# Linear attention with a gated output layer: a new order of TensorE work, loads parted from transposes, six output row buffers and a tail stored by two queues

## The chip, the cores and the metric

The kernel runs on one core of one Trainium2 chip. The metric is the device time of one execution in microseconds (us). The kernel before takes 238.62 us, the median of three timed runs (236.26 to 238.75). A single-core run is marked fast here when it lies within 1.5% of the fastest run of the same kernel in the same set, otherwise slow; a kernel run only once has no mark.

## The reference, cut to what matters

There are two parts. The first is linear attention, for 8 batches with 8 heads, 576 positions and head size 64. The second is a gated output layer of width 512 on its result.

```python
def phi(x):                                      # (b, h, 576, 64) -> (b, h, 576, 256)
    proj = np.einsum('bhsd,df->bhsf', x, w_phi)
    proj = proj - np.max(np.abs(proj), axis=-1, keepdims=True)
    return np.concatenate([np.exp(proj), np.exp(-proj)], axis=-1)
q_p, k_p = phi(q), phi(k)
kv  = np.einsum('bhsf,bhsd->bhfd', k_p, v);  z = np.sum(k_p, axis=2)
num = np.einsum('bhsf,bhfd->bhsd', q_p, kv)
den = np.einsum('bhsf,bhf->bhs', q_p, z)[..., None] + 1e-06
x   = (num / den).transpose(0, 2, 1, 3).reshape(8, 576, 512)
# gated layer: a causal convolution of 5 taps over positions gates x @ w_val
gate = sigmoid(sum over the taps of conv_w[k] * x shifted)
out  = (gate * (x @ w_val)) @ w_out
```

## The kernel before

The program is a list of some 1,040 tasks, one group of instructions each, written down in an order that was found beforehand (`ORDER`). Each engine carries out its own tasks strictly in that order. So a task that waits for a transfer holds up all later tasks of its engine.

For every batch from 2 on, GpSimd issues two loads, k and q (576 KB each). SyncE then issues a DMA transpose of each of them. The attention part projects k and q (`kp`, `qm`, `qp`), builds `kv` (`st`) and divides (`num`, `nrm`). Its result `XN` has to be transposed to `XT` for the gated part (`gate`, `val`, `out`). The batches in `XB` let a DMA do that, the others use TensorE and a copy by VectorE.

```python
XB = (3, 4, 5, 6, 7)                             # x is transposed by DMA in these batches
...
bufs = TT("KQN", 3, [P, NC, 2 * D])              # k and q as loaded: three buffers in turn
for b in range(1, B):
    for i, w in enumerate("kq"):
        self.N[w][b] = bufs[(2 * b + i) % 3]
...
def load(self, t, w, b):                         # GpSimd issues the loads of k and q
    o = self.N[w][b][:, :, :].rearrange("p y c -> p (y c)")
    ...
    self.nc.gpsimd.dma_start(o, self.rows(w, b))

def xpose(self, t, w, b):                        # SyncE issues their transposes
    self.nc.sync.dma_start_transpose(
        self.XT_[w][b % 2][:, :].rearrange("p (y c) -> p y c", c=P),
        self.N[w][b][:, :, :].rearrange("p y c -> p (y c)"))
...
def xtd(self, t, b, i):                          # x transposed by DMA
    self.nc.sync.dma_start_transpose(self.XT[b % 2][:, :, i, HALO:HALO + P], ...)

def xtp(self, t, b, i):                          # ... or by TensorE; i == 2 are the tail rows
    if i < 2:
        for h in range(H):
            nc.tensor.transpose(ps[:, h * P:(h + 1) * P], ..., self.ident[:, :])
    else:                                        # 16 transposes of 32x32
        for hh in range(4):
            for g in range(2):
                for par in range(2):
                    nc.tensor.transpose(ps[par * D:(par + 1) * D, hh * 32:(hh + 1) * 32], ...)
...
self.OUTS = TT("OUTS", 4, [P, DM], FP32)         # output rows: four buffers

def odma(self, t, b, c):                         # c == 4: the tail rows of two batches
    O = self.OUTS[out_seq(b, c) % 4]
    ...
        for i in range(2):
            for a in range(2):
                nc.sync.dma_start(d, O[p0:p0 + 32, :])
```

Of the kernel before, what the change touches and what calls it, by code (L numbers as in the profile page):

```python
# [26 lines left out]
XB = (3, 4, 5, 6, 7)  # L27
PIECES = 4
# [5 lines left out]
    "9:7:5 23:7:1 77:3:1 "  # L34
# [6 lines left out]
    "0 1 2 4 3 6 5 8 7 10 21 9 23 12 11 22 25 43 13 24 45 27 20 47 156 18 26 29 48 46 14 164 41 28 19 157 297 49 44 59 16 15 "  # L41
    "30 60 50 51 37 52 42 62 17 39 38 61 176 40 53 55 177 81 56 33 63 54 31 82 34 35 58 32 83 77 165 84 36 57 78 158 79 159 "
    "160 80 75 161 181 76 185 162 183 301 298 186 64 85 65 184 170 86 163 187 182 197 168 200 71 171 188 99 169 166 302 100 "
    "87 199 167 66 88 299 198 212 101 213 300 89 220 90 70 91 218 221 67 179 219 193 92 68 69 216 195 178 93 217 214 95 180 "
    "215 96 196 303 94 194 189 97 72 190 222 304 73 98 172 223 74 307 191 308 102 192 104 103 173 201 110 105 310 208 227 111 "
    "114 229 115 340 309 341 108 419 228 224 207 109 116 225 319 117 346 106 347 321 112 107 203 338 226 113 339 322 420 230 "
    "209 231 320 118 311 174 210 202 314 305 211 119 232 312 315 175 120 121 122 316 313 342 123 124 343 204 306 318 323 205 "
    "421 325 125 206 317 126 324 128 127 344 129 326 345 233 422 130 133 235 348 131 327 349 134 234 329 236 132 353 238 135 "
    "354 137 237 136 423 355 328 429 138 251 424 432 350 252 148 351 430 140 545 352 149 334 330 141 431 433 331 546 434 241 "
    "332 245 139 242 425 435 239 549 246 441 436 333 426 240 247 444 437 248 243 439 144 244 443 438 249 550 356 145 442 547 "  # L50
    "440 152 357 250 253 335 254 153 255 445 358 336 548 446 427 259 337 447 150 460 260 461 256 448 261 257 464 258 362 465 "
    "270 364 363 466 271 359 268 428 467 360 551 262 361 269 462 263 463 555 264 365 557 142 265 366 146 151 266 558 468 154 "
    "272 469 552 267 556 377 449 470 274 451 471 378 478 273 371 480 275 143 367 667 372 147 277 479 671 368 155 588 475 450 "
    "278 668 589 369 477 279 373 285 476 374 455 280 379 286 567 380 586 370 569 472 375 587 474 289 276 376 381 672 473 281 "
    "290 456 293 570 282 291 669 559 294 568 385 292 562 388 386 382 387 560 389 383 670 452 390 553 384 590 295 453 591 561 "
    "481 563 482 454 457 564 394 283 554 483 287 458 395 565 594 459 398 566 595 484 399 571 396 485 673 296 572 486 592 397 "
    "284 573 391 575 593 487 288 574 581 392 493 674 393 488 677 489 494 679 400 793 490 680 681 401 495 491 684 794 678 596 "
    "402 411 683 577 492 597 685 496 407 412 688 682 497 598 499 576 600 408 415 498 500 409 599 403 686 413 416 501 578 404 "
    "502 503 687 712 601 713 410 797 579 603 582 414 708 580 507 795 602 798 709 504 508 505 510 796 509 716 506 511 717 714 "
    "512 689 675 715 513 692 405 610 514 417 611 690 516 515 612 710 517 691 607 711 693 695 522 608 676 694 520 523 696 609 "  # L60
    "604 521 583 799 697 803 606 518 804 406 605 584 519 418 806 703 585 807 537 800 808 805 619 525 620 810 704 621 538 526 "
    "615 809 622 527 815 616 817 718 915 613 528 719 625 524 614 818 720 919 916 626 811 617 722 533 698 816 813 541 623 618 "
    "534 721 726 812 699 529 728 542 627 814 628 530 840 624 727 629 732 841 705 733 838 920 706 839 734 729 917 707 836 731 "
    "700 837 842 701 918 730 843 723 702 801 834 725 639 835 640 633 724 630 641 844 631 845 634 819 632 743 820 635 741 802 "
    "744 821 846 742 822 735 848 747 736 745 737 847 748 849 738 642 746 851 739 636 643 850 749 637 750 925 740 638 921 929 "
    "751 926 646 823 932 829 644 922 647 927 648 645 531 928 930 933 825 539 936 752 535 649 532 923 753 931 934 755 540 824 "
    "754 958 756 536 959 935 764 924 757 858 765 956 830 859 758 957 761 860 759 762 960 760 826 961 763 852 941 827 853 942 "
    "766 828 943 854 770 767 944 855 771 962 857 831 963 937 832 856 938 768 833 964 655 769 939 965 869 945 940 651 946 870 "
    "656 966 861 652 657 863 967 862 653 873 772 977 543 864 658 951 968 978 874 663 654 952 979 867 865 947 659 970 544 777 "
    "660 868 866 969 773 661 650 971 664 774 662 948 972 778 665 974 871 949 973 666 953 950 975 775 875 872 980 876 954 981 "  # L70
    "877 789 976 955 776 781 982 985 782 989 790 783 991 990 791 785 784 986 983 786 992 881 887 984 993 995 792 882 996 888 "
    "884 883 987 994 878 889 885 879 997 880 894 779 998 988 886 999 787 890 895 780 896 891 788 892 1006 893 1003 897 1000 "
    "1007 898 1009 1008 1001 1010 1004 911 1005 1002 899 1011 912 1016 900 913 1018 1017 901 914 1012 902 1014 1013 1019 907 "
    "1015 903 908 1020 909 1021 904 905 1033 1022 910 1023 1025 1034 906 1035 1029 1024 1037 1030 1036 1026 1031 1027 1038 "
    "1032 1039 1028 1040 "
)
FLEX = (
    "ADAADDAADDPPDPPDDADDAADDDDPPDPPDADADAPPAPPDADAAPPDPPDADDDDPPDPPDDAAAPPDPPADDAADPPDPPAAAAAPPDPDDAADAA"
)
BANKS = (  # L80
    "015441025023012345670167010123676742367672367672302301130167016723230167233424745010167230145452345010123234544567016745"
    "456752323550167452323452301232310245234567014567230167452350101230145010106723176745012323016701675674670101670101232367"
    "016767667454545236723452376723674501674501234005145676745452323236723014562345674545672323011230145012323014545540101450"
    "123674501010167670102367452367670101673452345452323012367047660167674523674501674523016456745010167232323067452301674545"
    "232316702367016723234567670123010676701452301230145467456701234501452377660"
# [69 lines left out]
def build(plan, em=None):  # L155
# [11 lines left out]
    def G(*k):  # L167
        return h.get(k)
# [4 lines left out]
    for b in range(B):  # L173
# [18 lines left out]
        for w in "kq":  # L192
            if b == 0:
                continue
            ld = A("l" + w, b, 0, "POOL", 0.75, fn("load", w, b), (seq[-3] if len(seq) >= 3 else []) + [hold[b] if b < 2 else None],
                   rank=-500 + (w == "q") if b == 1 else -980 if b == 0 else None, lat=0.6)
            h["ld" + w] = ld
            xf = A("l" + w, b, 0, "DMA", 3.8 if w == "k" else 3.5, None, [ld])
            dp = [xf]
            if w == "k":  # L200
                dp += [G("kp", b - 2, u) for u in range(NU)]
            else:
                dp += [G("qp", b - 2, u) for u in range(NU)] + [G("qm", b - 2, u) for u in range(NU)]
            if 0 < b <= PEB:
                tps = []
                for i, (c0, n) in enumerate(((0, 8), (8, 8), (16, 2))):
                    g = plan.group("tp", 1)
                    tp = h["sx" + w, b] = A("x" + w, b, i, "PE", 0.06 * n, fn("tp16", w, b, c0, n), dp, g, 0)
                    tps.append(tp)
                    x = A("x" + w, b, i, ("DVE", "ACT"), (dve(n * P), act(n * P)), fn("tc16", w, b, c0, n), [tp], g)  # L210
                    for u, (d0, m) in enumerate(UNITS):
                        if c0 <= d0 < c0 + n:
                            h["x" + w, b, u] = x
                seq.append(tps)
                continue
            x = h["sx" + w, b] = A("x" + w, b, 0, "SP", 2.7, fn("xpose", w, b), dp, rank=-700 if b == 0 else None, lat=-1.5)
            x = A("x" + w, b, 0, "DMA", 3.2, None, [x])
            seq.append([x])
            for u in range(NU):
                h["x" + w, b, u] = x  # L220
        if b == 1:
            cl = A("lk", 0, 0, "POOL", 1.7, fn("c_ld"), [hold[1]], rank=-450, lat=0.6)
            cx = A("lk", 0, 0, "DMA", 6.8, None, [cl], rank=-450)
            cd = A("lk", 0, 0, "SP", 0.8, fn("c_dup"), [cx], rank=-440)
            cx = A("lk", 0, 0, "DMA", 1.7, None, [cd], rank=-440)
# [595 lines left out]
```

## Time and profile before

| | before |
|---|---|
| timed runs, median | 238.62 us |
| the profiled run (marked slow) | 250.01 us, span 248.2 us |
| TensorE idle in its span | 248.2 - 206.3 = 41.9 us |
| mean granted TensorE clock | 0.928 |

The lines that the prediction rests on stand in it, with their reading. Two more views belong to the argument. The first is the list of DMA issues of the kernel before; the last number of a line is the median time in us from issue to landing:

```profile
KQN<-in_q_dram POOLq DMA_DIRECT2D x7, 576.0 KB, 11.3
...
XT<-XN SPq DMA_TRANSPOSE x10, 4.8
...
kT<-KQN SPq DMA_TRANSPOSE x6, 11.4
```

The second is the timeline of GpSimd and of SyncE's queue in the middle of the kernel before (start, duration, then what was issued):

```profile
70.50 0.60 POOL L497 DMA_DIRECT2D KQN<-in_q_dram  x1
...
69.23 5.13 SPq L512 DMA_TRANSPOSE qT<-KQN  x1
74.45 8.49 SPq L512 DMA_TRANSPOSE kT<-KQN  x1
```

The q load (70.50 us) is in flight while a q and a k transpose are carried out (69.23 to 82.94). The issue of one k transpose alone occupies SyncE's queue for 8.49 us.

### The profile page before, as it was taken

How to read it: one execution, taken by the hardware profiler on the slowest of the kernel's cores; microseconds unless marked ns; L12 is line 12 of the kernel's file. 1: busy time of each engine (PE TensorE's matmuls, PEld its weight loads, DVE VectorE, ACT ScalarE, POOL GpSimd, SP SyncE). 2: the span in 40 equal slices, each digit the busy share in tenths (PEclk: the TensorE clock that was granted, in tenths of full speed). 3: DMA queues.
4: the chain of work that ended last, by engine and by line, in shares of the span. 5: the costliest groups of instructions: out<-in, count | busy, mean ns of one | idle time of the engine just before them, and what ended most of it. 6: DMA issues, size and time to landing. Idle time of an engine off the chain costs nothing.

```text
span 248.2 us, 9200 instructions
## 1 busy us (share of the span) xinstructions
PE 206.3 (83%) x4033; PEld 144.7 (58%) x4047; DVE 173.8 (70%) x266; ACT 178.6 (72%) x258; POOL 102.2 (41%) x153
## 2 busy tenths in 40 slices
PE   6768877869979799997999898608999999799990
PEld 3545556646665577576665664504767876467640
DVE  2897799964786699968998789602898995264220
ACT  3888898977977586897899889801888969341440
POOL 5303999910980008902671079000087096001010
PEclk9995799997997999999999999955999999799998
DMA  6998978996599996999999999999498039284245
GB/s 211 322 223 128 191 224 132 203 263 103 87 138 154 206 241 156 208 209 278 163 187 99 313 168 136 76 54 296 45 212 260 3 115 168 66 136 123 85 145 151
DMA packets 55617, 41.43 MB, mean 167 GB/s; under 512 B 40026, under 2 KB 44890, under 8 KB 55514
## 3 DMA queue, kind: packets, MB, share of 16 engines
q1 hardware_dynamic: 49568, 31.46, 59.0%
q0 software_dynamic: 5760, 9.31, 26.0%
q8 instruction: 31, 0.51, 0.9%
q10 hardware_dynamic: 250, 0.09, 0.1%
q14 instruction: 8, 0.07, 0.1%
HBM read 30.49 MB, written 9.44 MB: 161 GB/s over the span
## 4 chain that ended last, share of the span: by engine, by line
PE 52%; DMA 13%; ACT 13%; DVE 12%; issue 7%; SPq 0%; ACTq 0%; DVEq 0%
PE PS L722 11%; PE PS L746 8%; DMA XT<-XN 7%; PE PS L703 7%; ACT QTIL L626 6%; PE PS L567 5%; PE PS L524 5%; ACT KTIL L541 5%; DMA out_dram<-OUTS 4%; PE PS L639 4%; DVE XN L660 3%; DVE MK L531 3%; PE PS L611 3%; PE PS L710 3%; PE PS L618 2%
## 5 line engine op out<-in xcount | busy, mean ns | idle before, releaser
L557 POOL TENSOR_TENSOR VT<-VN,EK 128x1152 bf16<-128x1152 f32 x31 | 65.8, 2123 | 55.5 <-ACT EK L550 42.6
L541 ACT ACTIVATE KTIL<-PS 128x1024 bf16<-128x1024 f32 (+1 forms) x80 | 73.5, 954 | 8.4 <-PE PS L524 5.4
L626 ACT ACTIVATE QTIL<-PS 128x1024 bf16<-128x1024 f32 x64 | 63.3, 1034 | 9.0 <-PE PS L618 6.8
L531 DVE TENSOR_REDUCE MQP<-PS 128x8 f32<-128x1024 f32 (+1 forms) x40 | 44.2, 1114 | 17.4 <-PE PS L524 14.6
L531 DVE TENSOR_REDUCE MK<-PS 128x8 f32<-128x1024 f32 (+1 forms) x40 | 44.1, 1111 | 5.2 <-PE PS L524 2.7
L714 ACT ACTIVATE TH<-PS 128x576 bf16<-128x576 f32 x32 | 19.9, 650 | 26.7 <-PE PS L710 25.9
L722 PE MATMUL PS<-XT,WV 64*128 64x288 bf16 x512 | 35.7, 283 | 0.2 <-DVE GV L728 0.2
L746 PE MATMUL PS<-WOUT,GV 128*128 128x512 bf16 x116 | 31.3, 395 | 1.0 <-issue 0.5
L728 DVE SCALAR_TENSOR_TENSOR GV<-TH,PS 128x576 bf16<-128x576 bf16 x32 | 23.7, 751 | 10.8 <-PE PS L722 10.1
L567 PE MATMUL PS<-VT,KTIL 64*128 64x65 bf16 x1152 | 25.5, 193 | 6.3 <-issue 5.9
L722 PEld LDWEIGHTS <-WV 64*128 64x128 bf16 x512 | 25.6, 94 | 6.2 <-issue 1.2
L567 PEld LDWEIGHTS <-KTIL 64*128 64x128 bf16 x1152 | 22.4, 96 | 8.3 <-issue 7.1
L524 PE MATMUL PS<-W,qT 64*128 64x128 bf16 x288 | 16.1, 223 | 11.4 <-issue 9.8
L703 PE MATMUL PS<-XT,GF 128*64 128x288 bf16 x256 | 22.9, 312 | 2.0 <-DMA XT<-XN 0.7
L691 POOL COPY XT<-XT 128x224 bf16<-128x224 bf16 x8 | 3.0, 373 | 48.7 <-DVE XT L687 48.7
L660 DVE TENSOR_TENSOR XN<-PS,RCP 128x512 bf16<-128x512 f32 x32 | 22.1, 691 | 1.1
L581 ACT ACTIVATE OUTS<-PS 128x512 f32<-128x512 f32 x21 | 12.4, 601 | 13.0 <-PE PS L746 7.0
L639 PE MATMUL PS<-KV,QTIL 128*128 128x65 bf16 x512 | 20.1, 195 | 1.7 <-issue 0.8
L639 PEld LDWEIGHTS <-QTIL 128*128 128x128 bf16 x512 | 18.4, 99 | 5.2 <-issue 2.8
L524 PE MATMUL PS<-W,kT 64*128 64x128 bf16 x288 | 16.3, 229 | 5.5 <-issue 2.0
L524 PEld LDWEIGHTS <-qT 64*128 64x128 bf16 x288 | 10.3, 96 | 16.0 <-issue 14.8
L746 PEld LDWEIGHTS <-GV 128*128 128x128 bf16 x128 | 11.5, 101 | 12.7 <-issue 2.2
(71 smaller groups left out, 249.5 us busy)
## 6 DMA issues: line engine op xcount, KB each, us to landing
VN<-in_v_dram SPq DMA_DIRECT2D x8, 1152.0 KB, 7.1
out_dram<-OUTS SPq DMA_DIRECT2D x32, 256.0 KB, 3.7
KQN<-in_k_dram POOLq DMA_DIRECT2D x7, 576.0 KB, 8.4
KQN<-in_q_dram POOLq DMA_DIRECT2D x7, 576.0 KB, 11.3
KTIL<-in_k_dram SPq DMA_DIRECT2D x4, 288.0 KB, 4.3
KTIL<-in_q_dram SPq DMA_DIRECT2D x4, 256.0 KB, 4.0
out_dram<-OUTS SPq DMA_DIRECT2D x16, 64.0 KB, 2.3
WV<-in_moe_w_val_dram POOLq DMA_DIRECT2D x1, 512.0 KB, 5.7
```

Of the source, the lines that this page charges most:

```text
L524: nc.tensor.matmul(self.PS[:, t.grp.banks[par], i * P:(i + 1) * P], X[rows, (c0 + i) * P:(c0 + i + 1) * P], self.W2[rows, :], start=True, ...
L531: self.nc.vector.tensor_reduce(o, self.two(t.grp, n * P).rearrange("p a (c f) -> p a c f", f=F), AX.X, ALU.max, apply_absolute_value=True)
L541: self.nc.scalar.activation(self.KTIL[b % 2][:, s, c0:c0 + n, :, :].rearrange("p c a f -> p a c f"), self.two(t.grp, n * P).rearrange("p a ...
L557: eng.tensor_tensor(self.VT[g][:, s, :, 0:D], self.VN[b % 2][:, NC * g:NC * g + NC, :], e.to_broadcast([P, NC, D]), ALU.mult)
L567: nc.tensor.matmul(self.PS[:, t.grp.banks[ab], (s * 2 + x) * E1:(s * 2 + x + 1) * E1], self.KTIL[b % 2][rows, s, J // 2, J % 2, :], self.V ...
L626: self.nc.scalar.activation(o, i, AF.Exp, scale=1.0 - 2.0 * s)
L639: nc.tensor.matmul(self.PS[:, t.grp.banks[h // 4], (h % 4) * E1:(h % 4 + 1) * E1], Q[:, s, c % 2, h, (c // 2) * P:(c // 2 + 1) * P], self. ...
L660: nc.vector.tensor_tensor(o.rearrange("p (g h) d -> p g h d", g=ng), n[:, :, :, 0:D], rc.unsqueeze(3).to_broadcast([P, ng, 4, D]), ALU.mult)
L703: self.nc.tensor.matmul(self.PS[h2 * D:(h2 + 1) * D, t.grp.banks[par], 0:R], self.GF[:, h, i, :], X[:, h, :, HALO - 8 * s:HALO - 8 * s + X ...
L722: nc.tensor.matmul(self.PS[:, t.grp.banks[par], 0:R], self.WV2[rows, h, j * P:(j + 1) * P], X[rows, h, :, HALO:XW], start=(h == 0), stop=( ...
L728: nc.vector.scalar_tensor_tensor(out=self.GV[b % 3][:, j, :, :], in0=self.TH[j][:, :, :], scalar=1.0, in1=self.two(t.grp, R), op0=ALU.add, ...
L746: nc.tensor.matmul(self.PS[:, t.grp.banks[0], :], lhsT, self.WOUT[:, j, :], start=(j == 0), stop=(j == 3))
```

## The change

The intent: tasks of dense and of sparse TensorE work alternate more closely. Loads of k and q and the DMA transposes no longer overlap (loads of v still may). Six of the ten DMA transposes of x go to TensorE. Six output buffers let evictions (copies of finished results out of PSUM) run ahead of the stores, and the last store is split over two queues. The two additional output buffers are paid for with the third buffer of k and q, and batch 1 borrows a part of `QTIL` instead.

```diff
-XB = (3, 4, 5, 6, 7)
+XB = (6, 7)
+NO = 6
 ORDER = ( ... another order of 1,050 tasks ... )
@@ loads and transposes of a batch
+    hx = A("lk", b, 0, "POOL", 0.15, fn("holdx", b - 1), [G("xq", b - 1, 0)])   # q of b-1 has been transposed
+    first = [hx]
+    ...                                              # w_out is loaded before batch 3, not at the start
+    for w in "qk":
+        ld = A("l" + w, b, 0, "POOL", 0.75, fn("load", w, b), first, ...)
+        first = [ld]
+    last = [xf["q"], xf["k"]]                        # both loads have landed
+    for w in "kq":
+        x = A("x" + w, b, 0, "SP", 2.7, fn("xpose", w, b), last + dp, lat=-1.5)
+        last = [x]
@@ DMA transposes of x only after the last load of k
-    xt = h["xtp", b, i] = A("xtp", b, i, "SP", 1.4, fn("xtd", b, i), nrms + war, lat=-0.2)
+    xt = h["xtp", b, i] = A("xtp", b, i, "SP", 1.4, fn("xtd", b, i), nrms + war + [G("xf", B - 1)], lat=-0.2)
@@ buffers
-        bufs = TT("KQN", 3, [P, NC, 2 * D])
+        bufs = TT("KQN", 2, [P, NC, 2 * D])
-        self.OUTS = TT("OUTS", 4, [P, DM], FP32)
+        self.OUTS = TT("OUTS", NO, [P, DM], FP32)
@@ tail rows of x: four whole transposes in place of sixteen small ones
+            for hh in range(4):
+                nc.tensor.transpose(ps[0:D, hh * P:(hh + 1) * P], self.XNT[:, hh, :], self.ident[:, :])
@@ GpSimd waits for the q transpose by reading one column of it
+    def holdx(self, t, b):
+        self.nc.gpsimd.tensor_copy(self.HOLD[:, :], self.XT_["q"][b % 2][:, NR - 1:NR])
@@ the last tail store
+        eng = nc.scalar if t.eng == "ACT" else nc.sync
-                    nc.sync.dma_start(d, O[p0:p0 + 32, :])
+                    eng.dma_start(d, O[p0:p0 + 32, :])
```

(Cut: the new order itself, the assignment of tasks to engines and PSUM banks, and two of the three warm-up groups, which go.)

## The prediction

> **What bounds the kernel now.** I began with the totals, the slices and the queues of the page, to see whether one engine is the limit.
>
> ```profile
> span 248.2 us, 9200 instructions
> PE 206.3 (83%) x4033; PEld 144.7 (58%) x4047; DVE 173.8 (70%) x266; ACT 178.6 (72%) x258; POOL 102.2 (41%) x153
> ...
> PEclk9995799997997999999999999955999999799998
> DMA  6998978996599996999999999999498039284245
> ...
> q1 hardware_dynamic: 49568, 31.46, 59.0%
> q0 software_dynamic: 5760, 9.31, 26.0%
> q8 instruction: 31, 0.51, 0.9%
> ```
>
> TensorE is the most used engine, but it is idle for 248.2 - 206.3 = 41.9 us, so the gain lies in its gaps. The profiled run took 250.01 us and is marked slow; the timed runs have a median of 238.62 us. 11.4 us of what this profile shows is therefore not in the number that I have to predict. Next, the waits of TensorE and a table of stages:
>
> ```profile
> PE PS L524 <- issue: 11.8, 4, 8.6
> PE PS L567 <- issue: 5.9, 5, 1.8
> ...
> PE PS L703 <- DMA XT<-XN: 0.7, 1, 0.7
> ```
>
> ```profile
> 0.00:60.00 60.00, 45.80 (x836) 32.30 (x839) 45.20 (x64) 47.96 (x66) 33.56 (x52) 0.89 0.92 207
> 60.00:150.00 90.00, 81.69 (x1702) 57.83 (x1704) 74.19 (x115) 74.81 (x109) 41.42 (x58) 0.98 1.00 180
> 150.00:176.00 26.00, 16.01 (x331) 10.53 (x332) 12.70 (x20) 13.56 (x21) 5.57 (x8) 0.74 1.09 136
> 176.00:220.00 44.00, 41.18 (x918) 30.51 (x920) 33.73 (x57) 32.90 (x49) 19.38 (x26) 0.96 0.59 131
> 220.00:248.20 28.20, 21.61 (x273) 13.48 (x267) 7.99 (x14) 9.33 (x16) 2.32 (x10) 0.97 0.51 124
> ```
>
> The reader is to see (columns: stretch, PE, PEld, DVE, ACT, POOL busy, clock, DMA share, GB/s) that the idle time of PE is 14.2 us in the first 60, 8.3 in the next 90, 10.0 in 150 to 176, 2.8 up to 220 and 6.6 at the end. From 60 to 150 PE is 91% busy: little is to be had there by reordering. "Issue" in the waits means that PE waited for nothing the profile names, and it accounts for 17.7 us of the idle time in nine gaps. I looked where these gaps fall in the timeline:
>
> ```profile
> 54.98 0.66 PE L567 MATMUL PS<-VT,KTIL 64*128 64x65 bf16 x25 [1.77 <-issue]
> ```
>
> ```profile
> 74.85 0.34 PE L524 MATMUL PS<-W,kT 64*128 64x128 bf16 x6 [1.64 <-issue]
> ```
>
> They fall in the middle of one group of matmuls (11 done, 25 to come; 2 done, 6 to come), where no semaphore is waited for. Counting PE instructions in program order, six of these gaps precede instructions 907, 1419, 2186, 2442, 3721 and 5511. Relative to 1419 that is -512, 0, 767, 1023, 2302 and 4092: multiples of 256 to within 4. And 31 packets of 0.51 MB on the instruction queue are 16 KB each, one per 256 instructions of 64 bytes. So PE starves at fetch boundaries while the DMA engines are full.
>
> The worst place is the chain of waits at 151 us:
>
> ```profile
> 150.31 0.87 SPq L678
> 151.24 17.51 DMA XT<-XN
> 168.89 1.17 PE PS L703 x8
> ```
>
> The two DMA transposes of x were issued at 149.58 us, between the loads of k (148.53) and q (150.06) of the last batch; they landed after 18.3 us against a median of 4.8. Three engines stood still for 8.6 us and the clock fell to 0.50.
>
> **What the Trainium skill says.** "Runtime: NRT & Kernel Launch", section "Instruction fetch mechanics": PE's stream is refilled in blocks of 16 KiB, 256 instructions, over a DMA queue of its own, "mostly hidden". The block size agrees with the 31 packets; "hidden" does not agree with gaps of 0.8 to 1.8 us. "DMA: Bandwidth & Descriptors", section "Issuing engines are not separate DMA queues": queues of all engines share the same 16 DMA engines, and issuing from several saves only sequencer time. The collision at 150 us agrees with the sharing. "TensorE: Matmul & The Clock Gate", Part 1: an idle window of about 3.4 us halves the clock. Agrees: 0.50 from 164 to 172 us. "Perfetto Trace Analysis", section "Optimization Strategy": interleave stages with different limits. The trace shows such stages: up to 60 us ACT and DVE are used as much as PE, from 220 us on PE runs alone.
>
> **The change part by part.** *Loads and transposes apart.* The q and k loads of batch b+1 now start when the q transpose of batch b has landed, and k and q transposes wait for both loads; w_out is loaded later, w_val earlier. The bytes stay. I expect the fetch gaps and late landings to shrink: of the 17.7 us of issue gaps, 8.6 belong to the jam, 9.1 remain; half of it, -4.5 us. The jam itself costs 8.6 us idle plus about 3 us (six us of work at half clock): 11.6, which is just the 11.4 us between profiled and timed runs. So I take it as nearly absent from the timed median and credit -1.5 us.
>
> *Transposes of x.* Six of ten go from DMA to PE (batches 3 to 5). 48 transposes by 4.0/48 = 0.084 us (x48, 4.0 us busy in the groups) are +4.0 us of PE; six copies of 0.68 us are +4.1 us of DVE. With PE at 91% in this stretch about 3 us of the 4.0 come onto the path: +3. DVE, at 82%, hides its share. Against this, x no longer waits 4.8 us for a landing but for about 0.6 + 0.7: -1.
>
> *Tail rows.* Per batch 16 transposes of 32x32 become 4 full ones (PE 2.4 us to 32 x 0.084 = 2.7 in all), while the copies grow from 16 of 0.22 us to 16 of about 0.35 us (estimate: 256 instead of 128 columns): +2.1 us DVE. 0 on the path.
>
> *Order.* The val matmuls of batch 0 stand at PE instruction 1268 instead of 1610, and w_val no longer arrives late (its second half is issued at 44.57 us before). Dense work therefore fills part of the 14.2 us of early idle: -2. Interleaving in the middle: at most the 8.3 us, less the fetch gaps counted: -1. Two single warm-up matmuls of about 0.6 us go, in a stage where PE waits anyway: 0.
>
> *Output.* Six buffers: ACT waited 2.5 us in three places for a store, the last two 1.35 and 0.49 us at the very end; -0.5 on the path. The last store: four issues took 2.48 us on one queue, two by two 1.24: -1.2.
>
> The sum: -4.5 - 1.5 + 3 - 1 - 2 - 1 - 0.5 - 1.2 = -8.7, so 238.6 - 8.7 = 229.9, taken as 230 us.
>
> **The rivals.** (a) *The DMA chain becomes the bound.* One batch now needs in series two loads (8.4 and 11.3 us to landing now, partly together), then two transposes (11.4 and 6.5): some 20 to 25 us, against a period of about 26 us before (q transposes issued at 88, 114 and 140 us) and about 25 wanted. There are only two instead of three buffers and less prefetch. For it: DMA share 1.00 from 60 to 150 us. Against it: those landings are long just because they overlap, and traffic is not added. If true, waits of kp on kT return every batch: 238 to 244 us. (b) *PE is the bound and fetch gaps stay*: they come with any load on the DMA engines, and stores and v loads stay; then only tail and order count while the transposes cost 3: 235 to 237 us. (c) *The jam is in the timed runs too*, the profile being slow for another reason: then taking it away gives up to 11 us more, 219 to 224 us.
>
> **Range and chances.** The sum has an error of some 6 us, mostly from the fetch gaps and the jam. (c) gets 0.2, (b) 0.18, (a) 0.08. Predicted 230 us, 8 in 10 between 221 and 237. Faster by 2% means below 233.8: 0.75; within 2%: 0.21; slower: 0.04.
>
> **What would show it.** Right: issue gaps of PE in sum below 9 us and none over 2; XT landings of at most 6 us; clock never at 0.5 after 60 us; PE busy about 206 us with 48 more transposes; under 5 us from PE's last matmul to the end. Wrong: PE waiting on kT or qT each batch, q and k transposes still landing after 10 us (rival a), or issue gaps unchanged (rival b). A profile of the changed kernel that agrees with its timed runs would support that the jam was what made the old profile slow.

## The result, and the profile after

| | before | after |
|---|---|---|
| median of the timed set | 238.69 us (236.26 to 240.55) | 228.54 us (227.03 to 232.16) |
| ratio of fast runs | 1 | 0.9586, 95% interval 0.9478 to 0.9694 |
| profiled run | 250.01 us, slow | 232.16 us, slow |

Ratios, here and below, are the mean time of one kernel's fast runs over that of the other's of the same rounds. They are thus not quite the ratio of the medians. The changed kernel is faster by 4.1%. Its profiled run is marked slow because it is 2% above the fastest run, but it is not the kind of run that the profile before was: nothing in it stood still for long.

The page of the changed kernel:

```profile
span 230.4 us, 9094 instructions
...
PE 200.5 (87%) x3981; PEld 142.5 (62%) x3997; DVE 178.7 (78%) x269; ACT 178.7 (78%) x261; POOL 103.1 (45%) x158
...
PEclk9999979979999999999999799999999999999999
```

TensorE is busy 200.5 us instead of 206.3, although it carries out 48 more transposes of x. The lowest slice of the clock after 60 us is 7, where it had been 5. The waits of TensorE (total, times, longest, in us):

```profile
PE PS L546 <- DMA kT<-KQN: 3.5, 1, 3.5
...
PE PS L546 <- issue: 2.1, 1, 2.1
```

The wait for nothing that the profile names was 17.7 us in two lines of the kernel before; it is 2.1 us in this one, with 0.9 and 0.5 in two further groups. A new wait stands at the top: 3.5 us for the k transpose of batch 2. It is a single wait, early in the timeline of TensorE:

```profile
45.03 0.72 PE L546 MATMUL PS<-W,kT 64*128 64x128 bf16 x16 [3.52 <-DMA kT<-KQN]
```

The stages of the changed kernel (stretch, then busy time of PE, PEld, DVE, ACT and POOL, clock, DMA share, GB/s):

```profile
0.00:60.00 60.00, 42.59 (x845) 31.51 (x847) 44.61 (x61) 48.16 (x68) 34.46 (x54) 0.94 0.93 205
60.00:150.00 90.00, 84.26 (x1698) 59.96 (x1703) 76.58 (x119) 77.77 (x117) 44.74 (x65) 0.98 0.92 196
150.00:200.00 50.00, 48.94 (x1118) 35.32 (x1123) 43.07 (x65) 45.90 (x69) 21.51 (x30) 1.00 0.52 125
200.00:230.40 30.40, 24.70 (x331) 15.69 (x328) 14.40 (x26) 6.83 (x12) 2.38 (x10) 0.99 0.47 120
```

TensorE's idle time is 17.4, 5.7, 1.1 and 5.7 us, in all 29.9. In the first 60 us it idles more than before (14.2), in all later stages less. (Idle time depends on the clock as well: in the first stage it is 0.94 here and was 0.89, and a gate matmul that takes 286 ns elsewhere (176 to 211 us before) takes 447 ns where the clock is 0.50 (169 to 174 us).) The landings:

```profile
kT<-KQN SPq DMA_TRANSPOSE x6, 5.2
...
XT<-XN SPq DMA_TRANSPOSE x4, 3.1
```

The k transposes land after 5.2 us instead of 11.4 (at most 6.5, the longest was 13.3; the traces have four of six landings), those of x after 3.1 instead of 4.8. The profile before was a slow run. In the fast one of the old order that comes below (b_x4pe) the medians are 8.1 and 3.7, so that against a fast run the shortening is smaller. The others have changed less: q transposes from 6.5 to 6.3, q loads from 11.3 to 8.7, k loads from 8.4 to 10.6. That the transposes no longer overlap with loads of k and q is seen in the timeline of SyncE's queue and of GpSimd:

```profile
65.71 2.65 SPq L534 DMA_TRANSPOSE qT<-KQN  x1
81.91 3.30 SPq L534 DMA_TRANSPOSE kT<-KQN  x1
...
72.57 0.61 POOL L519 DMA_DIRECT2D KQN<-in_q_dram  x1 [0.32 <-issue]
73.17 0.76 POOL L519 DMA_DIRECT2D KQN<-in_k_dram  x1
```

Both loads start after the q transpose of 65.71 us has landed, and the next k transpose starts after both loads. Issuing a transpose takes 2.7 and 3.3 us here instead of 5.1 to 8.5.

### The profile page after: what moved, and what is told of

It is laid out like the page before. It is cut to its first block, busy times and chain, and to the rows that moved or that the text cites. A ratio compares the mean times of both kernels' runs of the same rounds, so it can differ in the third digit from the quotient of the medians.

```text
span 230.4 us, 9094 instructions
## 1 busy us (share of the span) xinstructions
PE 200.5 (87%) x3981; PEld 142.5 (62%) x3997; DVE 178.7 (78%) x269; ACT 178.7 (78%) x261; POOL 103.1 (45%) x158
## 3 DMA queue, kind: packets, MB, share of 16 engines
q0 software_dynamic: 5760, 9.31, 23.9%
## 4 chain that ended last, share of the span: by engine, by line
PE 59%; DMA 10%; ACT 9%; DVE 9%; issue 5%; POOL 4%; SPq 1%; DVEq 0%; ACTq 0%
PE PS L742 14%; PE PS L766 10%; PE PS L589 7%; PE PS L723 6%; DMA QTIL<-in_k_dram 6%; PE PS L546 6%; PE PS L661 4%; ACT KTIL L563 4%; DVE MQP L553 3%; PE PS L633 3%; PE PS L690 3%; POOL VT L579 3%; PE PS L730 3%; DMA KTIL<-in_k_dram 2%; DMA kT<-KQN 2%
## 5 line engine op out<-in xcount | busy, mean ns | idle before, releaser
L563 ACT ACTIVATE KTIL<-PS 128x1024 bf16<-128x1024 f32 (+1 forms) x80 | 72.0, 948 | 9.9 <-PE PS L546 8.4
L766 PE MATMUL PS<-WOUT,GV 128*128 128x512 bf16 x113 | 30.5, 385 | 1.4 <-issue 0.9
L742 PEld LDWEIGHTS <-WV 64*128 64x128 bf16 x512 | 25.1, 94 | 7.1 <-issue 1.9
L546 PE MATMUL PS<-W,qT 64*128 64x128 bf16 x288 | 15.0, 221 | 6.2 <-issue 2.1
L723 PE MATMUL PS<-XT,GF 128*64 128x288 bf16 x256 | 20.1, 290 | 0.2
L546 PE MATMUL PS<-W,kT 64*128 64x128 bf16 x288 | 14.8, 223 | 6.3 <-DMA kT<-KQN 3.5
L603 ACT ACTIVATE OUTS<-PS 128x512 f32<-128x512 f32 x18 | 10.8, 609 | 8.8 <-PE PS L766 8.7
L546 PEld LDWEIGHTS <-qT 64*128 64x128 bf16 x288 | 9.7, 95 | 11.9 <-issue 9.6
L546 PEld LDWEIGHTS <-kT 64*128 64x128 bf16 x288 | 9.9, 96 | 10.5 <-issue 4.7
## 6 DMA issues: line engine op xcount, KB each, us to landing
KQN<-in_k_dram POOLq DMA_DIRECT2D x6, 576.0 KB, 10.6
```

The costliest lines, as they stand in the source:

```text
L546: nc.tensor.matmul(self.PS[:, t.grp.banks[par], i * P:(i + 1) * P], X[rows, (c0 + i) * P:(c0 + i + 1) * P], self.W2[rows, :], start=True, ...
L563: self.nc.scalar.activation(self.KTIL[b % 2][:, s, c0:c0 + n, :, :].rearrange("p c a f -> p a c f"), self.two(t.grp, n * P).rearrange("p a ...
L723: self.nc.tensor.matmul(self.PS[h2 * D:(h2 + 1) * D, t.grp.banks[par], 0:R], self.GF[:, h, i, :], X[:, h, :, HALO - 8 * s:HALO - 8 * s + X ...
L742: nc.tensor.matmul(self.PS[:, t.grp.banks[par], 0:R], self.WV2[rows, h, j * P:(j + 1) * P], X[rows, h, :, HALO:XW], start=(h == 0), stop=( ...
L766: nc.tensor.matmul(self.PS[:, t.grp.banks[0], :], lhsT, self.WOUT[:, j, :], start=(j == 0), stop=(j == 3))
```

## The experiments

Twelve kernels ran, in three sets of four, each set on another chip with eleven runs of the kernel before. "Old order" below means a kernel made from the one before, "new order" one made from the changed one.

"The jam" is the standstill of 8.6 us in the slow profile before (159 to 168 us); "fetch gaps" are the times in which TensorE waits for nothing but, by the theory, its next 256 instructions.

My theory after the result: TensorE's gaps at fetch boundaries were caused by loads and transposes in flight together; parting them takes most gaps away; the new order gains besides. Rivals: the gaps would have gone with any new order; the gain comes from the transposes of x, or from the output buffers; the jam of the slow runs was part of the time before.

### The jam, and the transposes of x in the old order

The first experiment takes the two DMA transposes away that jammed (those of batch 4) and lets TensorE do them. The second does so for batches 3 to 5, as the change does.

```diff
-XB = (3, 4, 5, 6, 7)
+XB = (3, 5, 6, 7)          # b_x4pe
+XB = (6, 7)                # b_x345pe; six (b_x4pe: three) tasks of the order move by some places
```

> The kernel before, with the two DMA transposes of x of batch 4 (those that landed after 18 us) done by PE and copied by DVE. Theory (the jam is only in the profiled execution): profile shortened to 238 to 243 us with no idle stretch over 3 us after 60 us, timed median unchanged, 236 to 240 us. Rival (the jam is in every execution): timed median falls to 227 to 232 us.

> The kernel before, with the six DMA transposes of x of batches 3 to 5 on PE and DVE, the one part of the change alone, in the old order. Theory: the PE work adds 3 us, later landings and fetch gaps give back 1 to 3: 236 to 241 us. Rival (the transposes on the DMA engines are what cost the kernel its time): 227 to 232 us, most of the change's gain.

With batch 4 changed, the four runs took 237.65 to 239.62 us, all fast. The ratio is 1.0008 (0.9906 to 1.0110): the fast runs do not contain a jam of 11 us. A part of one or two microseconds is not excluded, as the interval is 1% to each side and the 16 added transposes cost TensorE 5.3 - 4.0 = 1.3 us. Of the eleven runs of the kernel before on this chip, four took 251.74 to 255.49 us, like the profiled one of 250.01. In the two other sets none did.

With batches 3 to 5 changed the runs took 241.06 to 243.26 us, ratio 1.0150 (1.0063 to 1.0237). That is 3.6 us more than before, a little above the expected 236 to 241 us: in the old order the transposes of x cost on TensorE about what was predicted (+3 - 1) or more, and alone they gain nothing.

The first of the two also gives a profile of the old order in a fast run, to be compared with the changed kernel's; it has 16 of the 48 additional transposes in it. Its stages:

```profile
0.00:60.00 60.00, 46.03 (x841) 33.34 (x843) 45.69 (x64) 48.20 (x66) 33.61 (x52) 0.89 0.92 207
60.00:150.00 90.00, 83.49 (x1712) 59.17 (x1706) 74.55 (x116) 75.22 (x110) 43.43 (x60) 0.96 0.94 182
150.00:200.00 50.00, 46.29 (x1071) 34.13 (x1072) 42.08 (x65) 41.27 (x61) 22.61 (x30) 1.00 0.67 149
200.00:237.60 37.60, 29.61 (x459) 19.36 (x451) 13.25 (x26) 13.67 (x25) 2.90 (x12) 0.96 0.53 125
```

TensorE idles 14.0, 6.5, 3.7 and 8.0 us in it, together 32.2. I use these lines below in place of those of the slow run.

### Fetch gaps: do they belong to the program's count or to the work?

Sixty-four small matmuls that nothing uses, ahead of everything else, move all later TensorE instructions by 128 places, half a block.

```diff
+        for _ in range(64):
+            em.tiny()       # a matmul of 8 columns: 128 instructions with its weight load
```

> The kernel before, with 64 tiny matmuls (128 PE instructions) put ahead of the first one. Theory (the issue gaps of PE are instruction fetches every 256 instructions): the gaps over 0.8 us stand at the same counts from the start of the stream, so 128 instructions earlier in the program: before program instructions 779, 1291, 1547, 1803, 2059, 2314 and so on, or 128 later, and no longer after 11 of 36 and 32 of 36 matmuls of the state product of batches 1 and 2. Rival (gaps belong to what the program does there): they stay at those instructions of the program.

One look: 243.66 us. The gaps over half a microsecond in the timeline of TensorE:

```profile
58.47 0.19 PE L570 MATMUL PS<-VT,KTIL 64*128 64x65 bf16 x1 [2.09 <-issue]
113.85 0.44 PE L570 MATMUL PS<-VT,KTIL 64*128 64x65 bf16 x17 [0.61 <-issue]
159.45 0.30 PE L570 MATMUL PS<-VT,KTIL 64*128 64x65 bf16 x7 [2.62 <-issue]
186.94 2.77 PE L725 MATMUL PS<-XT,WV 64*128 64x288 bf16 x23 [2.73 <-issue]
```

They interrupt other groups than before, and other places in a group: before it was 11 matmuls done and 25 to come, here 35 and 1, 19 and 17, 29 and 7, 9 and 23. Counted in program order, each of the four gaps fits a place in a group near its time that lies at a boundary: after instructions 1675, 3721, 5511 and 6532. Relative to the 1419 of the prediction that is 256, 2302, 4092 and 5113, multiples of 256 to within 7. (A count of the records alone, which are complete in this trace and in that of b_out, gives 256, 2304, 4097 and 5119 after the same place.) Two of the numbers, 3721 and 5511, are gaps of the kernel before as well, with other work at them. So the gaps belong to the count: instruction fetch, as predicted. The count says only where a gap can be: of the six places named in advance, 1675 alone (before program instruction 1547) has one of over half a microsecond here.

The traces also hold each fetch, a packet of 16 KB on queue q8, which no view prints singly. Of the 44 gaps of this kind of at least 0.5 us in all fourteen profiles, 42 end 1.2 to 1.6 us after the end of such a packet; the exceptions are the jam (3.6) and the gap that ends at 136.94 us before (3.1). The packet itself is seldom slow (medians of 0.96 to 1.06 us): it comes late.

One of them was a surprise. The jam of the kernel before also ends at such a place: its 8.60 us come ahead of instruction 5511. In the next experiment, which leaves TensorE's program as it was, that place has 3.62 us:

```profile
160.77 0.28 PE L525 MATMUL PS<-W,qT 64*128 64x128 bf16 x1 [3.62 <-issue]
```

In b_x4pe, where instruction 5511 falls on other work and two transposes of x fewer are in flight, it is 0.90 us. The jam was thus not a thing apart. It was a fetch that met two loads and two DMA transposes of x (its packet took 4.04 us, no other one over 2.02), and its size differs between the profiles.

### Output buffers and the second queue alone, in the old order

```diff
-        self.OUTS = TT("OUTS", 4, [P, DM], FP32)
+        ox = T("OX", [P, 2 * DM], FP32)
+        self.OUTS = TT("OUTS", 4, [P, DM], FP32) + [ox[:, 0:DM], ox[:, DM:2 * DM]]
-        self.cw5 = T("cw5", [5, H, 2, D], FP32)
+        self.cw5 = ox[0:5, :].rearrange("t (h i d) -> t h i d", h=H, i=2)   # shares the space of two of them
-                    nc.sync.dma_start(d, O[p0:p0 + 32, :])
+                    (nc.scalar if b == B - 1 and i == 1 else nc.sync).dma_start(d, O[p0:p0 + 32, :])
```

> The kernel before, with six output row buffers and the last four tail stores issued by two queues, nothing else (the room comes from keeping the convolution weights in two of the output buffers at the start). Theory: 1.7 us less, 237.0 us (ratio 0.993). Rival (waits for output buffers hold up ACT and PE in the middle too): 3 to 5 us less, ratio 0.98 to 0.987.

Measured: 237.80 to 244.21 us, ratio 1.0004 (0.9901 to 1.0107). No gain is seen. The 1.7 us predicted are 0.7% and lie inside the interval, so they are neither shown nor excluded.

### Six buffers in the new order

```diff
-NO = 6
+NO = 4
-        eng = nc.scalar if t.eng == "ACT" else nc.sync
+        eng = nc.sync
```

> The changed kernel with four output buffers and one queue for the last stores. Theory after the same part alone did nothing in the old kernel: 0 to 1.5 us slower, 228.5 to 230 us. Rival (in the tighter kernel the buffers do bind): 231 us or more.

This run gave a wrong result (relative error 0.468) and is no fair measurement. The order of the changed kernel evicts up to six row groups before the first of them is stored; with four buffers an eviction writes over rows whose store has not been issued yet. (This is read from the program order.) It took 241.69 to 247.56 us, with a single wait of 5.7 us for an eviction. What follows is only that the new order cannot do without the six buffers: they are a condition of it, even if by themselves they gain nothing.

### The six transposes of x back on DMA, in the new order

```diff
-XB = (6, 7)
+XB = (3, 4, 5, 6, 7)
+                if i < 2 and 3 <= b <= 5:
+                    plan.group("xtp", 1)        # keeps the banks of all others as they are
```

> The changed kernel with the six transposes of x of batches 3 to 5 back on the DMA engines, at the same places of the order. Theory from the run that moved them in the old kernel (1.5% slower): PE is relieved of 3 to 4 us: 224 to 227 us. Rival (on the DMA engines they collide with loads and k and q transposes): 231 to 240 us, XT landings over 8 us.

Measured: 236.93 to 240.22 us, median 237.07, ratio 1.0108 (0.9870 to 1.0345). The next kernel ran on the same chip and keeps these transposes on TensorE: 0.9836. Between the two lie 2.8%, some 6 us, and in the direction opposite to the expected one. The theory that TensorE would be relieved by 3 us has fallen. Its largest wait:

```profile
PE PS L725 <- DMA XT<-XN: 4.4, 1, 4.4
...
129.62 2.13 PE L725 MATMUL PS<-XT,GF 128*64 128x288 bf16 x16 [4.35 <-DMA XT<-XN]
```

The gate matmuls of one batch now wait 4.4 us for the transposed x. In an engine that works strictly in order that holds up everything behind it. The rival that was named in advance, a collision, fits both the time (231 to 240 us) and the landings: the transpose awaited was issued at 120.05 us, while a k load (116.61 to 126.3) was in flight, and landed after 9.4 us; another that met a k load took 8.1 us. After 3.1 us, as in the changed kernel, it would have landed before the matmuls wanted it (at 125.3). a_free differs from a_xdma in the buffers and the hold too, so the 6 us are not the price of the transposes alone.

### Parting undone, first attempt

The hold on GpSimd is made to wait for nothing, and there are three buffers in turn again.

```diff
-        bufs = TT("KQN", 2, [P, NC, 2 * D])
+        bufs = TT("KQN", 3, [P, NC, 2 * D])        # used in turn; output buffers as in b_out
     def holdx(self, t, b):
-        self.nc.gpsimd.tensor_copy(self.HOLD[:, :], self.XT_["q"][b % 2][:, NR - 1:NR])
+        self.nc.gpsimd.tensor_copy(self.HOLD[:, :], self.ident[:, 0:1])
```

> The changed kernel with the parting of loads and transposes undone: three buffers in turn for k and q as before, and no wait of the loads for the q transpose of the batch before; order and all else as changed. Theory (parting them is what shortened landings and fetch gaps): landings of k and q transposes go back to 7 us and more, issue gaps of PE over 0.6 us come back, 231 to 235 us. Rival (the new order alone brings the gain): 227 to 230 us and no more gaps than in the changed kernel.

Measured: 230.54 to 232.73 us, ratio 0.9836 (0.9702 to 0.9969; only two runs of the kernel before count as fast in this set). The run missed its aim. Three of the five q loads from batch 3 on are issued at 72.55, 92.96 and 116.12 us, against 72.57, 92.47 and 115.52 in the changed kernel; the other two come 1.9 and 3.8 us earlier and overlap with a q transpose. What parts them is chiefly the place of the load in GpSimd's order, and the explicit wait adds little. The time lies in the range of the theory all the same, its median (231.79) some 3 us above those of the changed kernel on two other chips (228.54 and 228.97). The gaps did not come back (one, of 1.98 us), and the k transposes land after 6.2 us, not 7. So what the 3 us are stays open.

### Parting undone, second attempt

Besides the edit of a_free, the q load of each batch from 3 on moves in the order to a place ahead of the k transpose of the batch before it.

```diff
 ORDER
-  ... 199 222 301 195 ...    ... 206 107 422 310 ...
+  ... 199 222 422 301 195 ...   ... 206 107 310 ...      # task 422 is a q load; four more like it
```

> The changed kernel with three k and q buffers, and with the q load of batch b issued ahead of the k transpose of batch b-1, so that loads and transposes meet on the DMA engines in five batches (the run that only took the wait away left the loads at the same times). Theory (their meeting lengthens landings and starves PE): k transposes land after 8 us and more, issue gaps of PE over 4 us in sum, 231 to 236 us. Rival (PE, DVE and ACT have slack enough): as the changed kernel, within 1.5 us.

Measured: 244.92 to 252.86 us, ratio 1.0360 (1.0201 to 1.0520), 9% more than the changed kernel in the same set and far more than either theory gave. Its largest wait (two times, 11.2 us; one of 4.7 us for a q transpose follows):

```profile
PE PS L513 <- DMA kT<-KQN: 11.2, 2, 5.6
```

But the mechanism was not the expected one. The fetch gaps over half a microsecond come to only 2.2 us, and the one landing of a k transpose that the trace has took 4.7 us, no longer than in the changed kernel. The transposes are late because they are issued late: the earlier q load changes what the k load and the later loads have to wait for, as here on GpSimd:

```profile
87.76 0.54 POOL L486 DMA_DIRECT2D KQN<-in_q_dram  x1 [7.11 <-DMA KQN<-in_k_dram]
```

The k transposes then start at 77.44, 97.35 and 122.73 us, where the changed kernel has them at 62.87, 81.91 and 104.51. Where the moved q load did meet transposes, the issue of the q transpose took 8.30 and 6.10 us instead of about 2.7. The run therefore shows how much hangs on when a load is issued, and leaves open what the meeting alone costs in the new order.

### Parting alone, in the old order

Loads of k from batch 3 on are held until the q transpose of the batch before has landed; one task of the order moves so that this cannot deadlock.

```diff
+        if w == "k" and b > 2:
+            self.nc.gpsimd.tensor_copy(self.HOLD[:, :], self.XT_["q"][(b - 1) % 2][:, NR - 1:NR])
         self.nc.gpsimd.dma_start(o, self.rows(w, b))
```

> The kernel before, with each load of k and q from batch 3 on held until the q transpose of the batch before has landed (an explicit wait on GpSimd, one load moved behind it), old order and DMA transposes of x kept. Theory (parting alone shortens landings): 2 to 4 us faster than before, ratio 0.983 to 0.992, and no runs of 250 us. Rival (the old order needs the loads early): 3 us slower or more.

Measured: 243.52 to 250.31 us, ratio 1.0276 (1.0163 to 1.0390): slower by about 6.6 us. Its fetch gaps (a third, of 1.23 us, is at 206.96 us):

```profile
54.50 0.57 PE L535 MATMUL PS<-VT,KTIL 64*128 64x65 bf16 x25 [1.78 <-issue]
164.38 0.29 PE L492 MATMUL PS<-W,qT 64*128 64x128 bf16 x1 [5.63 <-issue]
```

Between 60 and 150 us the kernel before has five gaps of this size, 1.64 + 1.84 + 1.22 + 0.69 + 0.75 = 6.1 us; here it has none. TensorE's program differs in nothing that the count would notice. So with the loads parted the fetch gaps of this stage are gone, as far as one profile shows. But TensorE's idle time in the stage is 90 - 80.9 = 9.1 us, against 8.3 before: waits for transposes and for evictions have taken the place of the gaps (1.6 us for a q transpose, 2.3 us for an output buffer). And it jams at 164 us all the same, as the hold does not keep the transposes of x apart from the loads; one of its six runs took 250.31 us, where the theory had none. Up to 150 us TensorE idles hardly more than in the kernel before; the jam of 5.63 us, with 6.8 us at half clock from 161.8 us on, could by itself make up the 6.6 us. That the old order needs its loads early, as the rival has it, fits the time and is not shown.

### The new wait for batch 2 taken away

Batch 2's loads of q and k (tasks 297 and 299) are issued at 23.39 and 26.23 us in the changed kernel, and its k transpose at 39.84. In two kernels they come 13 to 17 us earlier, directly after w_val's load, or directly ahead of it.

```diff
 ORDER
-  ... 16 49 158 44 41 28 51 157 160 17 18 ...   ... 91 297 56 ...   ... 92 299 176 ...
+  ... 16 49 158 44 41 28 51 157 160 297 299 17 18 ...               # a_early: after w_val
+  ... 16 49 158 297 299 44 41 28 51 157 160 17 18 ...               # a_early2: ahead of w_val
```

> The changed kernel with the q and k loads of batch 2 issued right after that of w_val, 13 to 16 us earlier, ahead of the first products of v. Theory (the first 60 us wait for the k transpose of batch 2, 3.5 us of PE in the changed profile): 2 to 4 us faster than the changed kernel, 224 to 226.5 us. Rival (ACT and DVE set the pace of the first 60 us, or the earlier loads slow others): 227.5 to 230 us.

> The changed kernel with the q and k loads of batch 2 issued right after those of batch 1, ahead of that of w_val too. Theory: PE no longer waits for the k transpose of batch 2, 3 us faster than the changed kernel beside it. Rival (w_val and its copy now come late and hold up the queue of SyncE in front of the k transpose): no faster, or slower by up to 3 us.

And the changed kernel once more, unedited, beside the second of these:

> The changed kernel again, as the partner of the next three on the same chip. Both theories: 227 to 230 us, ratio to before 0.95 to 0.965; a second profile shows whether its few issue gaps (one of 2.1 us) were luck: theory, under 4 us in sum; rival, 6 us and more.

| kernel | runs, us | median | ratio to before (fast runs) |
|---|---|---|---|
| a_early | 223.85 to 227.35 | 225.15 | 0.9547 (0.9443 to 0.9650) |
| a_early2 | 224.73 to 226.91 | 225.99 | 0.9491 (0.9426 to 0.9555) |
| a_same | 225.12 to 235.80 | 228.97 | 0.9516 (0.9375 to 0.9658) |

Both are correct. The first two stages of a_early:

```profile
0.00:60.00 60.00, 45.28 (x912) 33.12 (x913) 48.30 (x68) 51.83 (x77) 36.99 (x57) 0.97 0.99 211
60.00:150.00 90.00, 87.15 (x1877) 62.62 (x1886) 79.17 (x121) 81.94 (x119) 44.14 (x66) 1.00 0.96 202
```

TensorE's idle time is 14.7 and 2.9 us here and 6.3 us in the rest, in all 222.1 - 198.2 = 23.9, and neither kernel has a wait for kT left among the larger ones. a_same shows that wait again, with 3.4 us, and 1.9 us of fetch gaps, so that their small number in the changed kernel was not luck.

On the chip where both ran, a_early2 is 3.0 us faster than a_same by the medians, and five of six runs of a_same are slower than all six of a_early2. By the fast runs alone (a_same has only two of these) the two are not told apart. That the wait is gone is shown; the 3 us are likely, and not settled at the level of the intervals. Both are the fastest kernels of this study, and both are clearly faster than the kernel before.

## Why the prediction was right or wrong

Predicted were 230 us and faster by over 2%; measured are 228.5 us. The total is right, and so is the mechanism of fetch gaps. Of the terms, several were mis-sized, one did not come and one had the wrong sign in the new order, so that part of the agreement is chance.

**The jam (-1.5).** Right in that it was nearly absent from the fast runs (1.0008); whether the 1.5 us were there cannot be told within 1%. Its nature was incomplete: the gap stands at a fetch boundary, instruction 5511, like the others. One reading was inexact: only the first of the two transposes was issued at 149.58 us, the second at 151.24, after the q load.

**Fetch gaps (-4.5 of 9.1).** Right in mechanism, and near in size. These are the gaps of at least 0.5 us, summed from the timelines of TensorE:

| old order | us | new order | us |
|---|---|---|---|
| before | 18.7 (8.6 of it the jam) | changed kernel | 2.6 |
| b_out | 13.1 | a_same | 1.9 |
| b_part | 8.6 | a_free | 2.0 |
| b_x345pe | 8.3 | a_xdma | 2.8 |
| b_shift | 8.1 | a_coll | 2.2 |
| b_x4pe | 7.0 | a_early2 | 1.7 |
| | | a_out4 | 1.2 |
| | | a_early | 0 |

From the fast profile of b_x4pe to the changed kernel the gaps fall by 7.0 - 2.6 = 4.4 us, from before without its jam by 10.1 - 2.6 = 7.5. All kernels of the new order have few gaps; of the old, all but b_part (three, 5.6 us of them the jam) have more. Which part of the change does it is only half settled: the rival that any new order would do it has not been tested, as there is only one. In the old order parting removed the gaps of the middle (b_part). In the new order letting one load overlap with transposes did not bring them back (a_coll). As a term of its own "loads and transposes apart" does not show a gain: alone, in the old order, the run was 6.6 us slower. That it pays together with the new order is likely (a_free, where it is undone in part, is some 3 us slower, on another chip) and not shown.

**Transposes of x (+3 - 1).** This is the step that failed. The operations were sized well: 96 of them take 8.2 us instead of 4.0 for 48, and twelve copies 8.1 us instead of 4.0 for six.

```profile
L690 PE MATMUL PS<-ident,XN 128*128 128x128 bf16 x96 | 8.2, 235 | 0.5 <-issue 0.5
```

(After the bar: busy us, mean ns of one, idle time before.) In the old order the result is near the predicted one, +3.6 us (the two terms together were +2). In the new order the same move is worth about 6 us in the other direction (a_xdma against a_free). The prediction took the term from the stage table of the old order and added it to another order, in which x on DMA meets the k loads and brings the wait of 4.4 us (before, all waits for it were 0.7 us). A cost that depends on the order can't be added up that way.

**Order, early part (-2).** It did not come. The val matmuls do come earlier, but TensorE's idle time in the first 60 us rose from 14.2 to 17.4 us. As an estimate of the work done, busy time by clock is 45.80 x 0.89 = 40.8 us before and 42.59 x 0.94 = 40.0 after: no gain, rather a loss of about 1 us. The k transpose of batch 2 came too late by 3.5 us; this is rival (a), the chain of loads and transposes, in one place instead of every batch. a_early takes it away; the stage idles 14.7 us, and 45.28 x 0.97 = 43.9 us of work are done in it.

**Order, middle and end (-1).** Too small. From 60 us on, b_x4pe idles 18.2 us, the changed kernel 12.5. Of these 5.7 us, 5.8 - 2.6 = 3.2 are fetch gaps (one of b_x4pe's, of 1.2 us, lies before 60 us); the other 2.5 contain the output terms too.

**A term that was missing: the clock.** TensorE's busy time was taken as fixed, with 206 us expected. It fell to 200.5 with more transposes in it. Busy time multiplied by the mean clock of the span is nearly the same in three profiles: 205.4 x 0.951 = 195.4 (b_x4pe), 200.5 x 0.976 = 195.7 (changed), 198.2 x 0.987 = 195.6 (a_early). Over all fourteen it lies between 191.4 (before) and 197.5 (b_x345pe). The mean clock of the fast runs of the kernel before is 0.958 (nine runs of two sets), of the changed kernel 0.973 (five). As an estimate from these, 195.6/0.958 - 195.6/0.973 is about 3 us. But that is less than the spread of the product, the gate matmuls took only 1.56 times as long at 0.50 (447 against 286 ns) and not twice, and two fast runs of the changed kernel took 228.44 and 228.64 us at 0.985 and 0.956, where the same working would have them 6 us apart. So the size of this term stays open. The traces do show where clock is lost: in stretches at 0.50, most of them 3.4 us long. Before, apart from the start and the end, three begin within 1 us after a fetch gap (55.3, 75.8 and 212.3 us) and one of 13.7 us begins in the jam. In the changed kernel there are three before the end: one follows the wait for the k transpose (45.4 us), one the gap of 2.07 us (127.3), one is early (31.8). These gaps are of 1.39 to 2.07 us, shorter than the 3.4 us of which the prediction speaks. Not every gap has such a stretch after it (none follows 83.52 us before). A part of this term thus belongs to the gaps and that wait, and is not beside them.

**Tail rows (0) and output (-0.5 - 1.2).** The 32 whole transposes take 3.2 us instead of the 2.4 us that the 128 small ones took, a little more than the 2.7 estimated; the copies take 0.28 us each and not 0.35. The gain of the buffers and the second queue was not seen alone (b_out). In the profiles the time from TensorE's last matmul to the end is 248.2 - 241.9 = 6.3 us before and 5.6 after. Over all profiles of one queue in the old order it is 6.2 to 7.0 us (five), with two queues 4.9 to 5.8 (eight). So of -1.2 some 0.6 to 0.9 are seen.

**The marks that were set in advance.** Issue gaps below 9 us in sum: yes. None over 2: one of 2.07, just missed. XT landings of at most 6 us: yes, at most 3.8. The clock not at 0.5 after 60 us: no. The slices of the page, which are means, do not fall below 0.7, but from 127.30 to 130.70 us it is 0.50. Busy time of 206: no, 200.5. Under 5 us from the last matmul to the end: no, 5.6.

In sum, the agreement of the total (8.7 us predicted, about 10 measured) is partly luck: the early stage gave nothing, the later stages gave more, and the record does not divide the gain among the new order, the parting and the clock.

## What to carry to other kernels

An idle engine that waits for no semaphore, in the middle of a group of equal instructions, may be waiting for its own instructions: count its instructions up to the gap, and look at what the DMA engines carry at that time and whether the clock falls after it. Do not add up the worth of parts of a reordering from the old profile: the same move of transposes to TensorE cost 1.5% in one order and went with a gain of 2.8% in the other. After a reordering look at the first stage by itself, for a load issued late there shows as a single wait, which here was removed by moving two entries of the order.

## What the Trainium skill lacked or had wrong

- "Runtime: NRT & Kernel Launch", section "Instruction fetch mechanics", calls the crossing of a block "mostly hidden". The block size of 256 instructions is confirmed by b_shift, but in the old order three to nine of some 31 crossings had gaps of over 0.5 us, of 0.6 to 3.6 us each and up to 8.6 us in a jam; in sum 7.0 to 18.7 us of a 240 us kernel, and 0 to 2.8 us in the new order. The DMA engines were mostly busy then, but not always: in the gap of 2.73 us of b_shift (184.20 to 186.94 us) their share was 0.03. The page does not say how such a gap is recognised.
- "DMA: Bandwidth & Descriptors", section "DMA Transpose (X-bar)", has no duration of a transpose beside plain loads. Here transposes of x landed 3.1 to 3.8 us after their issue in the changed kernel, where no load of k or q was in flight, and up to 18.3 us in the one before, where two were; the issue of a k or q transpose occupied SyncE's queue for 2.4 to 4.5 us in the changed kernel and for up to 11.3 us in the one before.
